# One priority per operation in place of two numbers per kind, and 20 warm-up matmuls in place of 38, in a list-scheduled kernel

## The chip, the cores and the metric

The kernel runs on one core of one Trainium2 chip. The metric is the device time of one execution in microseconds (us), and I quote medians. Most executions of one kernel agree within a per cent or so. An execution more than 1.5% above the fastest of its kernel is called slow and is left out of every ratio, though not out of the medians.

## The reference

The kernel computes a gated block on x of 2048 rows by 640 columns (S by D). One branch is a feed-forward network, 640 to 1728 to 640. The other is a convolution over all 2048 rows, done as a Fourier transform in two steps.

```python
def A_ref(q, k, v, shift_k, ssm_k, ssm_D):
    kv = shift_conv(k, shift_k) * v          # 4 taps along S
    y = irfft(rfft(pad(kv)) * rfft(pad(ssm_k)))[:S]
    return q * (y + kv * ssm_D)
def B_ref(x, w1, b1, w2, b2):
    return gelu(x @ w1 + b1) @ w2 + b2
xn = layernorm(x)
out = x + A_ref(xn, k, v, shift_k, ssm_k, ssm_D) * silu(B_ref(xn, w1, b1, w2, b2))
```

The output is x plus a small product.

## The kernel before

Nothing in the kernel is in a fixed order. While the program is built, each piece of work is handed to `plan.op` with its engine, an estimated cost, and the buffers it reads and writes. A list scheduler then plays the program on a model of the chip, and each engine's instructions are emitted in the order of the planned starts.

```python
LAT = {"PE": 0.2, "ACT": 0.15, "DVE": 0.13, "POOL": 0.15, "SP": 0.0}
MODE_SWITCH = 0.095
# ... cut
    def schedule(self):
        # ... cut: dependences and buffer slots
        for k, os in kinds.items():
            a, b = self.due[k]
            for i, o in enumerate(os):
                o.prio = -(a + (b - a) * i / max(1, len(os) - 1))
        # ... cut: for every ready operation o and every engine e it may use
                    t = max(est, free[e])
                    c = o.cost[e]
                    p = o.prio
                    # ... cut: penalties for a table load or a change of array shape
                    key = (t, -p, c)
                    if best is None or key < best[0]:
                        best = (key, o, e, t, c, slots)
        # ... cut: the winner o starts at t and ends at end
            if o.dma:
                dma_free = max(dma_free, end + 0.65) + o.dma / o.rate
                o.done = dma_free + 1.4
            else:
                o.done = end + LAT[e]
        # ... cut
        order.sort(key=lambda o: (o.start, o.i))
        return order
    def emit(self):
        for o in self.schedule():
            o.fn(o.eng)
DUE = {
    "b1": (-2658.69, -12.83), "cab0": (8557.17, 6667.77), # ... cut, a pair of numbers for each kind
}
```

The key is first the start time `t` and only then the priority, so a priority decides only between operations that could start at the same moment. All transfers share one line, first in, first out: a transfer begins when every earlier one has ended, at 330 KB per us.

The parts that the argument touches:

```python
    op("DVE", 0.14, lambda e: nc.vector.memset(b1_r[:], 0.0), writes=[b1r_b], kind="first")
    for i in range(38):   # warm-up
        op("PE", 0.22, ...matmul of 128x128 by 128x512..., kind="warm")
    def load(fn, nbytes, ...):      # at most four loads in flight: a pool of 4 tokens
    def load_rows(e):               # small loads issued by ScalarE, b1_r in two pieces
    # second half (h = 1) of k and v: lies where kT lay, so it waits for all users of kT
    def load_k(h, i): ... eng="POOL", extra=list(kT_b.users) if h else []
    def load_v(h, i): ... eng="POOL", extra=list(kT_b.users) if h else []
    # first transform step: two matmul pairs, evicted to an io tile, stored to DRAM scratch
    def f1_pair(i, h, src, src_b, scr, scr_b, kind):
        o = Buf(pool=io_pool, parts=2)               # one of four io tiles
        # ... cut: matmuls to psa buffers, evictions by ACT|DVE
        op("SP", 0.46, lambda e: nc.sync.dma_start(out=by_n2(scr[h], i), in_=o.v...), dma=P * 4 * D)
    # per group: read scratch K and U, second step (F2), product, inverse (I1)
    def middle(h, g):
        pr = [Buf(pool=io_pool) for _ in range(2)]   # the same four io tiles
        op("DVE", 0.735, prod, reads=[uin, kk[a]], writes=[pr[a]], ...)
```

The products and the stores of the first step share the four io tiles. The matmuls of the transform share three psa buffers in PSUM.

Of the kernel before, what the change touches and what calls it, by code (L numbers as in the profile page):

```python
# [64 lines left out]

LAT = {"PE": 0.2, "ACT": 0.15, "DVE": 0.13, "POOL": 0.15, "SP": 0.0}
TABLE_LOAD = 1.28
MODE_SWITCH = 0.095

class Plan:  # L70
    def __init__(self, due):
# [41 lines left out]
    def schedule(self):  # L113
        ops = self.ops
        succ = {o: [] for o in ops}
        for o in ops:
            for d in o.deps:
                succ[d].append(o)
        follow = {o: [] for o in ops}
        for o in ops:  # L120
            for d in o.after:
                follow[d].append(o)
        kinds = {}
        for o in ops:
            kinds.setdefault(o.kind, []).append(o)
        for k, os in kinds.items():
            a, b = self.due[k]
            for i, o in enumerate(os):
                o.prio = -(a + (b - a) * i / max(1, len(os) - 1))
        for o in ops:  # L130
            o.left = len(o.deps) + len(o.after)
            o.est = 0.0
            o.done = None
        free = {"PE": 1.0, "ACT": 1.0, "DVE": 1.0, "POOL": 1.0, "SP": 1.0}
        dma_free, table, mode = 0.0, None, 0
        for p in {b.pool for o in ops for b in o.allocs}:
            p.reset()
        ready = [o for o in ops if o.left == 0]
        order = []
        while ready:  # L140
            best = None
            for o in ready:
                est, slots, ok = o.est, [], True
                for b in o.allocs:
                    cand = None
                    if b.pool.fifo and b.seq != b.pool.next:
                        ok = False
                        break
                    for s in b.pool.slots:
                        if any(s is c for c in slots) or any(u.done is None for h in s[1] for u in h.users):  # L150
                            continue
                        t = max([u.done for h in s[1] for u in h.users], default=0.0)
                        if cand is None or t < cand[0]:
                            cand = (t, s)
                    if cand is None:
                        ok = False
                        break
                    est = max(est, cand[0])
                    slots.append(cand[1])
                if not ok:  # L160
                    continue
                for e in o.engs:
                    t = max(est, free[e])
                    c = o.cost[e]
                    p = o.prio
                    if e == "ACT" and o.table is not None and o.table != table:
                        c += TABLE_LOAD
                        p -= self.due["switch"][0]
                    if e == "PE" and o.mode != mode:
                        c += MODE_SWITCH  # L170
                        p -= self.due["mode"][0]
                    if e != o.engs[0]:
                        wait, less = self.due["dve" if e == "DVE" else "pool"]
                        if max(est, free[o.engs[0]]) <= t + wait:
                            continue
                        p -= less
# [3 lines that stand above are left out]
            assert best is not None, [(o.kind, o.i) for o in ready]  # L180
            key, o, e, t, c, slots = best
            for b, s in zip(o.allocs, slots):
                b.v = s[0]
                b.pool.next += 1
                s[1] = [b]
            o.eng, o.start = e, t
            end = t + c
            free[e] = end
            if e == "ACT" and o.table is not None:
                table = o.table  # L190
            if e == "PE":
                mode = o.mode
# [5 lines that stand above are left out]
            ready.remove(o)  # L198
            order.append(o)
            for s, t in [(s, o.done) for s in succ[o]] + [(s, o.start) for s in follow[o]]:  # L200
                s.left -= 1
                s.est = max(s.est, t)
                if s.left == 0:
                    ready.append(s)
        assert len(order) == len(ops), "the plan cannot run"
        order.sort(key=lambda o: (o.start, o.i))
        self.span = max(o.done for o in ops)
        return order
# [2 lines left out]
        for o in self.schedule():  # L211
            o.fn(o.eng)

DUE = {
    "b1": (-2658.69, -12.83), "cab0": (8557.17, 6667.77), "cab1": (-1486.18, -152.64), "cst0": (-305.42, 2707.06),
    "cst1": (-2821.97, -4792.38), "dve": (0.47, 30.2), "f1_0": (-871.05, 1734.66), "f1_1": (1301.71, 4641.74),
    "f1_2": (1114.17, 1732.61), "f1_3": (2717.88, 2832.21), "f1k0": (-526.64, -1917.59), "f1k1": (-45.43, 1009.63),
    "f1u0": (-4387.08, -5449.77), "f1u1": (-871.6, -2537.05), "f2_0": (-101.73, 568.69), "f2_1": (55.74, -1410.81),
    "f2_2": (2347.64, 580.24), "f2_3": (1367.74, 4253.7), "f2k0": (-4800.76, 938.43), "f2k1": (1474.47, -1695.6),
    "f2u0": (1087.17, -104.99), "f2u1": (-2201.6, -388.99), "fin0": (3005.36, 3026.91), "fin1": (4769.18, 4253.19),  # L220
    "first": (-4156.08, -3068.36), "gtab": (-2228.31, -2211.96), "halo1": (3569.33, 2410.81),
    "i10": (-236.08, -1811.7), "i11": (-1708.64, -1347.6), "i20": (2541.11, 1052.7), "i21": (2701.42, 3183.93),
    "kin0": (-593.69, 758.66), "kin1": (1951.88, -1170.69), "kt": (-677.48, -1093.47), "kv0": (-3727.38, -6497.24),
    "kv1": (818.93, -2911.39), "ln0": (-2934.3, -4187.58), "ln1": (-6791.26, -5326.47), "ln2": (1941.49, 937),
    "ln3": (896.12, -1662.13), "load1": (-2919.94, -4066.71), "load10": (1978.17, 919.81),
    "load11": (-2440.26, -3260.22), "load12": (4122.04, 8470.58), "load13": (7611.05, 3845.84),
    "load14": (3186.96, 908.54), "load15": (4188.27, 3598.3), "load16": (-1111.28, -467.99),
    "load17": (3134.69, 3049.36), "load18": (376.5, 3182.36), "load19": (1982.23, 428.93),
    "load2": (-5152.92, -6327.1), "load20": (5478.92, 7432.46), "load21": (-2345.4, 472.84),
    "load22": (-3453.91, -1273.89), "load23": (3030.08, 3625.43), "load24": (-2431.86, -3878.73),  # L230
    "load3": (-4653.66, -5026.1), "load4": (-4049.51, -2679.33), "load5": (-3127.18, -2370.67),
    "load6": (-1295.43, -2222.83), "load7": (-3086.77, -1734.57), "load8": (-486.48, 2101.2),
    "load9": (1995.94, 1552.87), "mode": (197.93, 0), "ones1": (-1676.37, -2952), "pool": (7.25, -13.8),
    "prod0": (69.2, -3781.34), "prod1": (2713.4, -508.43), "small": (-2624, 2474.77), "switch": (23.42, 0),
    "uin0": (-5019.36, -4445.98), "uin1": (-4066.58, -3058.07), "warm": (-9990.03, -8766.04),
    "wexp": (462.86, 314.56), "wtab": (-4840.89, -4511.51), "xt0": (-2587.15, -3103.92), "xt1": (191.84, -3623.5),
    "xt2": (1912.14, 2825.82), "xt3": (-3593.86, -3830.63),
}

@with_exitstack  # L240
def kernel(
# [75 lines left out]
    psf_t = [psum.tile([P, 512], F32, name="psf%d" % i) for i in range(2)]  # L317
    psa_t = [psum.tile([P, 2, 512], F32, name="psa%d" % i) for i in range(3)]

    plan = Plan(DUE)  # L320
    op = plan.op

    def evict(e, out_, in_):
# [12 lines left out]
    kf_b = Buf(parts=DT)  # L336
# [5 lines left out]
    row_b, dD_b, b1r_b, b1_b, id_b, bias_b = Buf(), Buf(), Buf(), Buf(), Buf(), Buf()  # L342
# [17 lines left out]

    warm_b = Buf()
    op("DVE", 0.2, lambda e: nc.vector.memset(hT_t[0][:, FT - 2, :], 0.0), writes=[warm_b], kind="first")
    for i in range(38):
        ps = Buf(pool=psf)
        op("PE", 0.22, lambda e, ps=ps: nc.tensor.matmul(out=ps.v[:, :], lhsT=hT_t[0][:, FT - 2, 0:P], rhs=hT_t[0][:, FT - 2, :],  # L365
                                                         start=True, stop=True),
           reads=[warm_b], writes=[ps], kind="warm")
# [16 lines left out]
    for q in range(CH):  # L384
        load(lambda e, q=q: nc.sync.dma_start(out=x_b[0].v[:, q, :], in_=x_v[:, q, :]), P * D * 2,
             writes=[x_b[0][2 * q], x_b[0][2 * q + 1]])
# [233 lines left out]
    for t in range(DT):  # L620
# [8 lines left out]
            o = ps.v[:].rearrange("p a b -> p (a b)").bitcast(BF16).rearrange("p (a b) -> p a b", b=P)  # L629
            evict(e, kT[:, h * 8:(h + 1) * 8, t * P:(t + 1) * P], o[:, h * 8:(h + 1) * 8, :])  # L630

        op("PE", 1.4, ktr, reads=[kf_b[t], id_b], writes=[ps], kind="kt")
        for h in range(2):
            op("ACT|DVE", (0.905, 0.6), lambda e, h=h, kev=kev: kev(e, h), reads=[ps],
               writes=[kT_b[2 * t + h]], kind="kt")
# [282 lines left out]
```

## Time and profile before

| | before |
|---|---|
| time, median of the first 3 runs | 211.09 us |
| profiled span | 208.5 us |
| useful TensorE work in it | 173.2 us |
| lost by 45 us (the head) | 17.7 us |
| 92 changes of array shape at 0.107 us | 9.8 us |
| other losses from 45 us to the last matmul (the body) | 3.0 us |
| tail after the last matmul | 4.8 us |

Useful work is counted as the prediction below explains it.

### The profile page before, as it was taken

What the parts mean: (1) busy time and instruction counts of PE and PEld (TensorE: products, weight loads), DVE (VectorE), ACT (ScalarE), POOL (GpSimd) and SP (SyncE); (2) the same over time, 40 slices, a digit from 0 to 9 for tenths busy, and PEclk for the clock granted to TensorE, in tenths of its full rate; (3) what the DMA queues carried; (4) which work ended last, traced back from release to release, by engine and by line L of the source; (5) the groups of instructions that cost most, each with busy time, mean ns of one, the idle gap of its engine ahead of it and who ended that gap; (6) DMA issues with size and microseconds to landing.
All of it is one profiled execution on the core that took longest, in us unless ns stands there. A gap on an engine that the chain in (4) does not pass through costs nothing.

```text
span 208.5 us, 5242 instructions
## 1 busy us (share of the span) xinstructions
PE 197.8 (95%) x2091; PEld 109.5 (53%) x2091; DVE 162.2 (78%) x301; ACT 148.2 (71%) x232; POOL 44.5 (21%) x67
## 2 busy tenths in 40 slices
PE   7997999989999999989999999999999899999990
PEld 2483446557676444334335666666643343667670
DVE  8879699999995543749899999562496676869993
ACT  2859879987787998769999776564579899830100
POOL 8992357400000001901201111001002021120000
PEclk9998899999999999999999999999999999999998
DMA  5999998993469899999964734896799963127994
GB/s 167 354 402 375 337 392 271 385 241 120 189 157 293 311 266 396 328 327 246 336 171 130 230 136 156 241 252 166 234 336 371 290 199 128 66 92 241 331 338 139
DMA packets 46137, 52.85 MB, mean 253 GB/s; under 512 B 14352, under 2 KB 35503, under 8 KB 46112
## 3 DMA queue, kind: packets, MB, share of 16 engines
q1 hardware_dynamic: 41920, 37.10, 58.0%
q0 software_dynamic: 4160, 15.40, 21.0%
q8 instruction: 16, 0.26, 0.5%
q14 instruction: 9, 0.07, 0.1%
q10 hardware_dynamic: 32, 0.01, 0.0%
HBM read 31.14 MB, written 18.35 MB: 237 GB/s over the span
## 4 chain that ended last, share of the span: by engine, by line
PE 66%; DVE 23%; DMA 6%; ACT 2%; issue 1%; SPq 0%; DVEq 0%
PE psf_105 L603 12%; PE psf_106 L603 11%; PE psf_106 L568 11%; PE psf_105 L568 9%; DVE GAB L689 5%; DVE stats L500 4%; DMA kv_90<-scrU_66 4%; DVE GAB L696 3%; DMA kv_90<-scrU_65 3%; PE psf_105 L365 3%; PE psf_106 L365 2%; PE psa_109 L851 2%; PE psa_108 L851 2%; PE psa_107 L816 2%; DVE xreg L520 2%; DVE xreg L878 2%
## 5 line engine op out<-in xcount | busy, mean ns | idle before, releaser
L568 PEld LDWEIGHTS <-w_sb 128*128 128x128 bf16 x280 | 25.1, 98 | 33.2 <-issue 9.0
L568 PE MATMUL psf_106<-hx_93,w_sb 128*128 128x512 bf16 x105 | 27.2, 391 | 0.8 <-ACT hx_93 L324 0.8
L568 PE MATMUL psf_105<-hx_93,w_sb 128*128 128x512 bf16 x105 | 26.2, 380 | 1.1 <-ACT hx_93 L573 1.1
L603 PEld LDWEIGHTS <-hx_93 128*128 128x128 bf16 x224 | 21.5, 98 | 9.4 <-issue 1.1
L603 PEld LDWEIGHTS <-hx_94 128*128 128x128 bf16 x224 | 21.7, 98 | 8.9 <-issue 0.5
L696 DVE TENSOR_TENSOR GAB<-GAB 128x1280 bf16<-128x1280 bf16 x24 | 19.6, 817 | 0.0
L603 PE MATMUL psf_105<-w_sb,hx_93 128*128 128x320 bf16 x112 | 16.6, 299 | 0.0
L603 PE MATMUL psf_106<-w_sb,hx_93 128*128 128x320 bf16 x112 | 16.6, 299 | 0.0
L603 PE MATMUL psf_105<-w_sb,hx_94 128*128 128x320 bf16 x112 | 16.6, 299 | 0.0
L603 PE MATMUL psf_106<-w_sb,hx_94 128*128 128x320 bf16 x112 | 16.5, 299 | 0.0
L858 POOL DMA_DIRECT2D scrC_67<-kv_90 x8 | 6.0, 754 | 49.0 <-ACT kv_90 L324 29.5
L500 DVE BATCH_NORM_STATS2 stats<-xreg 128x6 f32<-128x320 bf16 x32 | 13.7, 471 | 0.3 <-DMA xreg<-in_A_q_dram 0.2
L858 POOL DMA_DIRECT2D scrC_68<-kv_90 x8 | 6.0, 752 | 37.4 <-DVE kv_90 L324 15.2
L689 DVE TENSOR_TENSOR GAB<-kv_91,w_exp 128x1280 bf16<-128x1280 bf16 x16 | 13.0, 821 | 0.1
L689 DVE TENSOR_TENSOR GAB<-kv_90,w_exp 128x1280 bf16<-128x1280 bf16 x16 | 12.9, 818 | 0.0
L324 ACT CAST kv_90<-psa_108 128x640 bf16<-128x640 f32 x18 | 12.6, 701 | 0.4 <-PE psa_108 L851 0.3
L573 ACT ACTIVATE hx_93<-psf_105,b_f 128x512 bf16<-128x512 f32 (+1 forms) x14 | 9.9, 706 | 3.1 <-PE psf_105 L568 3.1
L816 PEld LDWEIGHTS <-F2m 64*32 64x32 bf16 x512 | 5.2, 89 | 12.9 <-issue 11.7
L573 ACT ACTIVATE hx_93<-psf_106,b_f 128x512 bf16<-128x512 f32 x14 | 9.8, 704 | 2.4 <-PE psf_106 L568 2.3
L324 ACT CAST kv_90<-psa_109 128x640 bf16<-128x640 f32 x15 | 10.4, 695 | 1.0 <-PE psa_108 L816 0.4
L418 POOL DMA_DIRECT2D kv_91<-in_A_v_dram x2 | 1.8, 915 | 43.2 <-ACT kk_96 L324 38.8
L573 ACT ACTIVATE hx_94<-psf_106,b_f 128x512 bf16<-128x512 f32 x14 | 9.7, 696 | 1.6 <-PE psf_106 L568 1.0
(191 smaller groups left out, 451.4 us busy)
## 6 DMA issues: line engine op xcount, KB each, us to landing
hx_94<-in_A_ssm_k_dram SPq DMA_DIRECT2D x5, 512.0 KB, 6.7
kv_90<-scrU_65 SPq DMA_DIRECT2D x8, 320.0 KB, 5.1
scrC_67<-kv_90 POOLq DMA_DIRECT2D x8, 320.0 KB, 5.5
kv_90<-scrU_66 SPq DMA_DIRECT2D x8, 320.0 KB, 4.5
kv_91<-scrC_67 SPq DMA_DIRECT2D x8, 320.0 KB, 5.0
scrC_68<-kv_90 POOLq DMA_DIRECT2D x8, 320.0 KB, 3.7
out_dram<-xreg SPq DMA_DIRECT2D x16, 160.0 KB, 4.5
kv_91<-scrC_68 SPq DMA_DIRECT2D x8, 320.0 KB, 4.8
```

The lines of the kernel that those rows point to most:

```text
L324: (nc.scalar.copy if e == "ACT" else nc.vector.tensor_copy)(out=out_, in_=in_)
L365: op("PE", 0.22, lambda e, ps=ps: nc.tensor.matmul(out=ps.v[:, :], lhsT=hT_t[0][:, FT - 2, 0:P], rhs=hT_t[0][:, FT - 2, :], start=True, st ...
L500: nc.vector.bn_stats(out=stats[:, c, j, h, :], in_=x_b[c].v[:, j, h * H:(h + 1) * H])
L520: nc.vector.tensor_scalar(out=o, in0=i, scalar1=rstd[:, c, j:j + 1], scalar2=nmr[:, c, j:j + 1], op0=ALU.mult, op1=ALU.add)
L568: nc.tensor.matmul(out=o, lhsT=w1_sb[:, t, ft * P:(ft + 1) * P], rhs=xnT_b[c].v[:, :, t, :], start=(t == 0), stop=(t == DT - 1))
L573: op("ACT", 0.575, lambda e: nc.scalar.activation(out=hT_b[c].v[0:M, ft, :], in_=ps.v[0:M, :], func=ACT.Gelu_apprx_tanh, bias=b1_f[0:M, ft ...
L603: nc.tensor.matmul(out=ps.v[:, 0:H], lhsT=hT_b[c].v[0:M, ft, q * P:(q + 1) * P], rhs=w2_sb[0:M, ft, hs], start=(ft == 0), stop=(ft == FT - 1))
L689: nc.vector.tensor_tensor(out=out_, in0=k_all[h][:, r + 3 - j:r + 3 - j + KR, :], in1=w_exp[:, j, None, hs].to_broadcast([P, KR, H]), op=A ...
L696: op("DVE", 0.735, lambda e, t=t: nc.vector.tensor_tensor(out=a.v, in0=a.v, in1=t.v, op=ALU.add), reads=[t], writes=[a], kind="kv%d" % h)
L816: nc.tensor.matmul(out=ps.v[t * 32:t * 32 + 32, r, 0:H], lhsT=F2m[r * Q:r * Q + Q, z * 32:z * 32 + 32], rhs=src[r * Q:r * Q + Q, t, :], st ...
L851: nc.tensor.matmul(out=pc[t // 2].v[r * Q:r * Q + Q, t % 2, 0:H], lhsT=I1m[t * 32:t * 32 + 32, w, :], rhs=pr[a].v[t * 32:t * 32 + 32, 2 * ...
L858: op("POOL", 0.85, lambda e: nc.gpsimd.dma_start(out=by_group(scrC[h], g), in_=cs.v), reads=[cs], writes=[scrC_b[h][g]], kind="cst%d" % h, ...
```

## The change

The intent is to give the schedule search more freedom: each operation gets its own priority, the engine of an eviction can be fixed, the cost of a change of array shape depends on the shape that is left, and the warm-up is shorter. The work itself is not touched.

```diff
-MODE_SWITCH = 0.095
+MODE_SWITCH = (0.093, 0.115, 0.137)
@@
-        kinds = {}
         for o in ops:
-            kinds.setdefault(o.kind, []).append(o)
-        for k, os in kinds.items():
-            a, b = self.due[k]
-            for i, o in enumerate(os):
-                o.prio = -(a + (b - a) * i / max(1, len(os) - 1))
+            o.prio, o.force = self.due["ops"][o.i]
@@
                 for e in o.engs:
+                    if o.force >= 0 and len(o.engs) > 1 and e != o.engs[o.force]:
+                        continue
@@
-                        c += MODE_SWITCH
+                        c += MODE_SWITCH[mode]
@@
-                    if e != o.engs[0]:
+                    if e != o.engs[0] and o.force < 0:
@@
-DUE = {
-    "b1": (-2658.69, -12.83), "cab0": (8557.17, 6667.77), ... cut
+ORDER = {
+    "dve": (1.0, 6.24), "switch": (1.83, 0.0), "pool": (9.83, -4.05), "mode": (0.98, 0.0),
+    "ops": (
+        (-29.7, -1), (-51.76, -1), (-35.76, -1), (-11.15, -1), ... cut, one pair for each operation
@@
-    for i in range(38):
+    for i in range(20):
@@
-        op("PE", 1.4, ktr, reads=[kf_b[t], id_b], writes=[ps], kind="kt")
+        op("PE", 1.0, ktr, reads=[kf_b[t], id_b], writes=[ps], kind="kt")
```

## The prediction

> **What bounds the kernel now.** I read the page's busy table and slices first, then the per-window sums, then the start times in the timeline, and last the waits. The page:
>
> ```profile
> PE 197.8 (95%) x2091; PEld 109.5 (53%) x2091; DVE 162.2 (78%) x301; ACT 148.2 (71%) x232; POOL 44.5 (21%) x67
> ...
> PE   7997999989999999989999999999999899999990
> ...
> PEclk9998899999999999999999999999999999999998
> ```
>
> TensorE (PE) is busy in every slice but the first and last, so the kernel is a TensorE queue with a head and a tail, and a new order can only save what that queue loses. Busy time hides the losses, since it counts warm-ups, cold-clock matmuls and pipelined ends. So I counted useful time from distances between starts in the timeline: FFN1 280 matmuls at 0.2157 us (60.4 us); FFN2 448 at 0.136 (60.9); the 128 WA/WB matmuls at 0.136 (17.4); the 64 GA/GB ones at 0.136 (8.7); 64 batches of eight F2 matmuls at 0.147 (9.4); 16 inverse batches at 0.55 (8.8); 80 ssm_k transposes at 0.064 (5.1); input transposes and w_exp 2.4. Together **173.1 us** of the 208.5 us span. The other 35.4 us, place by place:
>
> Head: the first useful matmul starts at 11.67 us. By 45 us only 27.2 us of useful work has been issued, so 17.8 us are lost there.
>
> ```profile
> 11.36 0.38 PE L365 MATMUL psf_106<-hx_93 128*128 128x512 bf16 x1
> ...
> 11.67 0.18 PE L490 MATMUL psf_105<-ident,b_r 14*128 14x14 bf16 x1
> ...
> 11.78 0.72 PE L626 MATMUL psa_107<-ident,hx_94 128*128 128x128 bf16 x8
> 11.88 0.17 DVE L492 CAST b_f<-psf_105 128x14 f32<-128x14 bf16 x1 [1.79 <-PE psf_105 L490]
> ```
>
> L365 is a warm-up; the tiny bias transpose L490 and the ssm_k transposes L626 stand behind all 38 of them, and even VectorE (DVE) waits 1.79 us for that transpose. The window sums show the second half of the head:
>
> ```profile
> 11.00:12.00 1.00, 1.00 (x8) 0.44 (x7) 0.12 (x2) 0.69 (x1) 1.00 (x3) 1.00 0.98 410
> 17.00:18.00 1.00, 0.57 (x8) 0.33 (x6) 1.00 (x2) 0.74 (x2) 0.20 (x1) 1.00 1.05 373
> 18.00:19.00 1.00, 0.74 (x4) 0.38 (x4) 0.97 (x4) 1.00 (x3) 0.00 (x0) 0.97 1.06 380
> 19.00:20.00 1.00, 0.34 (x1) 0.10 (x1) 1.00 (x3) 1.00 (x3) 0.00 (x0) 0.50 0.99 367
> 20.00:21.00 1.00, 1.00 (x4) 0.41 (x3) 0.97 (x4) 1.00 (x3) 0.00 (x0) 0.50 1.04 387
> ```
>
> The columns are PE, PEld, DVE, ACT, POOL, granted clock, DMA share, GB/s. TensorE starves at 17 to 20 us while the DMA engines are full; then its clock is halved from 18.9 to 22.4 us, just as FFN1 begins.
>
> Body: from 45 us to the last matmul at 203.4 us, 158.4 us pass for 145.8 us of useful work, a loss of 12.6 us. Most of it are changes of array shape:
>
> ```profile
> 69.21 0.30 PE L669 MATMUL psa_107<-kv_91,WA 128*128 128x320 bf16 x1
> ...
> 70.03 1.24 PE L568 MATMUL psf_105<-hx_93,w_sb 128*128 128x512 bf16 x5
> 71.20 0.33 PE L816 MATMUL psa_107<-kin_97,F2m 64*32 64x320 bf16 x8
> 71.35 0.32 PE L816 MATMUL psa_109<-kin_97,F2m 64*32 64x320 bf16 x8
> 71.60 0.31 PE L669 MATMUL psa_108<-kv_91,WA 128*128 128x320 bf16 x1
> ```
>
> Five FFN1 matmuls occupy 1.08 us before another full-array matmul, but 1.17 us (70.03 to 71.20) before a 64*32 one; the second F2 batch takes 0.25 us to the next full one where the first took 0.15. So about 0.10 us each way. The trace has 92 such changes; without waits I take 0.107 us each: 9.8 us. That leaves 2.8 us of true gaps in the body, waits for scrU reads among them.
>
> Tail: from 203.4 to 208.5 us, 5.1 us: SiLU, multiply, add and the last store.
>
> Check: 17.8 + 9.8 + 2.8 + 5.1 = 35.5. The measured median, 211.09 us, is 2.6 us above the span, and I keep that offset.
>
> **What the Trainium skill says.** "TensorE: Matmul & The Clock Gate", Part 1, describes a gate that grants half clock until a window of about 3.4 us has been busy, and takes it back after an idle one. The trace agrees: warm-ups start 0.43 us apart until 5.3 us and 0.216 us apart after, and the half-clock stretch lasts 3.4 us. So 20 warm-ups are enough to open the gate; what is risked is an idle window after them. The same page's Part 4 says that transposes do not count as busy for this gate; here the clock stayed at 1.00 through 48 transposes from 11.8 to 14.8 us, so this trace doesn't show it. Part 3 says that matmuls keep strict program order, which is why L490 cannot pass the warm-ups; the 1.79 us wait agrees. The skill's root page, "Trainium Kernel Development and Optimization", Key Constraints, says that DMAs issued by different engines share the same 16 DMA engines: the DMA share near 1.0 agrees, so in the head only the order of loads can help. I found no page that prices a change of array shape.
>
> **The change part by part.**
>
> 1. 18 warm-ups go. Each is 0.216 us, 3.9 us in all, so they end at about 7.7 us and not 11.6. The first ssm_k tile landed at 7.69 us (the next two at 9.40 and 10.67), and x was normalised from 12.2 us, behind VectorE's wait for L490. So some useful work can start 2 to 4 us earlier, but thinly. Estimate: 2 us.
>
> 2. The load order. In the table the three w1 loads have priorities of about 49 to 55, all loads of k and v on POOL but one about -30, the ssm_k loads -5. In the old kernel the first w1 load issued at 7.86 us and landed at 16.62, so FFN1 could not begin before then. FFN1 of chunk 0 now has priorities 3 to -41, ahead of most of the early convolution. This should fill the 17 to 20 us hole (2.6 us idle or at half clock). Against it I set a probable half-clock window after the shorter warm-up (3.4 us, costing 1.7). Estimate: net 2 us.
>
> 3. Shape changes. Corrected switch costs let the search group better. But the three psa buffers allow at most three F2 batches in a row, and the runs of F2 already average 64/33 = 1.9 batches. I take 92 down to 84: 0.8 us.
>
> 4. The rest of the order: one number per operation instead of a line per kind. Of the 2.8 us gaps and 5.1 us tail I give it 1 us. FFN2 of the last chunk and the GA/GB products carry the lowest priorities together (to -223), so the tail looks the same: one SiLU chain after TensorE's last.
>
> 5. The work itself is unchanged: 173.1 us. The forced choice of ACT or DVE for evictions moves work between engines with 71% and 78% and should cost nothing. Scheduling runs while the program is built; the ktr cost of 1.0 is only a number for it.
>
> Sum: 2 + 2 + 0.8 + 1 = 5.8 us, which I round to **6 us**: a span near 202.5 and a time of 205.0 us.
>
> **The rivals.**
>
> A. The warm-ups were hidden anyway: data, not warm-ups, set the head. For it: DMA is full from 7 to 20 us and ssm_k lands from 7.7 on. Against it: VectorE's 1.79 us wait and FFN1's late weights are matters of order. Time: about 209.5.
>
> B. The clock gate takes it back. With nothing useful from 7.7 to 11 us a window could pass idle, and two windows at half clock (3.4 us lost) cancel the gain. For it: the gate closed at 18.9 us after only one thin stretch. Time: 208 to 210.
>
> C. The plan fits its model, not the chip: the penalty for changing shape falls from 198 in a range of 18500 (1.1%) to 0.98 in a range of 278 (0.35%), so the changes could grow; 20 more would cost 2.1 us, and only 7 of the 32 F2 pairs have priorities within 1 of each other. Together with VectorE, which was busy for nearly all of 32 to 57 us, as a new bound for the convolution input, the time would be 208 to 212.
>
> D. All goes well: head lag down to 12.5 us, 76 changes, gaps 1.5, tail 4.5: span 199.7, time 202.
>
> **Range and chances.** The floor of D and rivals A to C give 201.3 to 209.2 as the range. Faster by over 2% means under 206.9 us: the 6 us must come to at least 4.2. I give that 0.63, within 2% 0.33, slower by over 2% (above 215.3) 0.04, as the body is almost gapless and little else can get worse.
>
> **What would show it.** Step 1: the first useful matmul before 9 us and no VectorE wait for L490 above 0.5 us. Step 2: the first w1 load lands before 12 us, FFN1 starts before 16 us, and useful work issued by 45 us is above 30 us (27.2 now); the clock row shows at most one half-clock window after the first. Step 3: 78 to 90 shape changes. Step 4: the last matmul within 4 to 5.5 us of the end. I am wrong if the useful work by 45 us stays near 27 us, if changes exceed 100, or if long TensorE waits appear between 45 and 200 us.

## More of the kernel before

The window sums of the kernel before, for the stretch that turns out to matter. The columns are the window, its length, busy time and instructions of TensorE (PE), its weight loads, VectorE (DVE), ScalarE (ACT) and GpSimd (POOL), then the granted clock, the share of the DMA engines, and GB/s.

```profile
85.00:90.00 5.00, 5.00 (x31) 2.18 (x30) 3.57 (x5) 3.73 (x6) 3.29 (x5) 1.00 1.02 330
90.00:95.00 5.00, 4.37 (x77) 1.61 (x75) 2.89 (x4) 3.33 (x7) 0.00 (x0) 1.00 1.16 305
95.00:100.00 5.00, 5.00 (x102) 2.16 (x87) 4.83 (x7) 4.68 (x9) 1.51 (x2) 1.00 1.09 245
```

TensorE is busy although the DMA engines are full, and the clock stays at 1.00. These are the microseconds in which the second half of k and v is loaded.

The timeline of ScalarE in the head of the kernel before (start, duration, engine, line, what, then the idle time before it and what ended it):

```profile
1.54 0.32 ACTq L379 DMA_DIRECT2D b_r<-in_B_b_dram  x1
...
5.76 2.00 ACT L467 ACTIVATE WB<-w_sb,sin_bias 128x2048 bf16<-128x2048 int32 x1 [2.27 <-DVE w_sb L465]
```

ScalarE has issued its small loads before 2.2 us, and its first table function, a table of sines, starts at 5.76.

## The result

| | before | after |
|---|---|---|
| time, median (range), 4 runs each | 210.67 us (209.30 to 211.23) | 219.55 us (217.97 to 220.67) |
| profiled span | 208.5 us | 216.2 us |
| head loss | 17.7 | 16.7 |
| shape changes | 92, 9.8 us | 82, 8.8 us |
| other body losses | 3.0 | 11.9 |
| of these, from 80 to 110 us | 1.0 | 9.3 |
| tail | 4.8 | 5.6 |

The changed kernel is **slower**: the ratio is 1.043, with a 95% interval of 1.033 to 1.052. Every ratio here is the mean time of one kernel's fast runs over that of the other's in the same rounds, so it is not quite the ratio of the quoted medians. The prediction, 205.0 us in 201.3 to 209.2, was wrong.

The loss table says where to look. The head gained 1.0 us and the shape changes 1.0, while 8.9 us were lost in the body and 0.8 in the tail. The sum, +7.7 us, is the difference of the spans. The page of the changed kernel shows the place at a glance:

```profile
PE 195.9 (91%) x2073; PEld 109.6 (51%) x2073; DVE 163.4 (76%) x301; ACT 149.7 (69%) x233; POOL 47.3 (22%) x67
...
PE   7829999999999999728999999999999999999980
...
PEclk9988999999999999995999999999999999999996
DMA  5998999669948699994469952495979995216994
```

Each digit is 5.4 us. TensorE has a hole at digits 17 and 18, counted from 0 (from 91.9 to 102.7 us), and its clock drops in the second of them. The DMA row has 9s in digits 14 to 17 and falls to 4 in digit 18, so the hole **begins while the DMA engines are full**. The windows (the columns as before):

```profile
85.00:90.00 5.00, 3.66 (x53) 1.50 (x53) 1.66 (x3) 2.92 (x6) 1.79 (x3) 1.00 1.01 351
90.00:95.00 5.00, 3.27 (x50) 1.14 (x49) 1.46 (x2) 2.65 (x4) 0.00 (x0) 1.00 1.03 395
95.00:100.00 5.00, 1.81 (x12) 0.70 (x12) 3.32 (x5) 1.27 (x2) 0.78 (x1) 0.68 0.41 143
100.00:105.00 5.00, 5.00 (x45) 1.49 (x50) 3.89 (x6) 2.05 (x5) 0.00 (x0) 0.63 0.82 212
```

TensorE, VectorE and ScalarE are all less busy than before in the first three windows. In the first two the DMA share is 1.0, so a wait for data is the first thing to look for. In the last window TensorE looks fully busy, but its clock is halved for most of it, from 96.8 to 103.7 us. The waits of TensorE, longest first (instruction, what it waited for, total us, times, longest):

```profile
PE psa_107 L918 <- DVE kv_90 L426: 4.8, 1, 4.8
PE psa_109 L728 <- ACT w_exp L426: 3.1, 1, 3.1
...
PE psa_109 L918 <- DMA kv_90<-scrU_65: 1.3, 1, 1.3
```

The second is in the head, at 15.6 us. The first is in the hole: a batch of F2 matmuls (L918) waits for VectorE's eviction (L426), which frees its psa buffer. Why was VectorE late? Its timeline, and the chain of waits around it:

```profile
96.58 0.83 DVE L942 TENSOR_TENSOR io_101<-kk_95,kv_90 128x1280 bf16<-128x1280 bf16 x1 [5.12 <-DMA scrK_64<-io_101]
97.32 0.82 DVE L426 CAST kv_90<-psa_107 128x640 bf16<-128x640 f32 x1
```

```profile
84.59 11.87 DMA scrK_64<-io_101
...
98.19 0.47 PE psa_107 L918 x8
```

This is read backwards. The F2 batch starts at 98.19, after the eviction of 97.32. The inverse matmuls (L953) had filled that psa buffer by about 92.0 us, so the eviction could have run then. But in VectorE's queue a product (L942) stands ahead of it. The product writes tile io_101, and that tile is still being stored to scratch: the store was issued at 84.59 and ran **11.87 us**. VectorE idled 5.12 us, and TensorE 4.76 us.

ScalarE can evict too, and it was idle at that time:

```profile
98.73 0.69 ACT L426 CAST kv_90<-psa_107 128x640 bf16<-128x640 f32 x1 [4.83 <-PE psa_107 L918]
```

But the eviction of 97.32 is operation 601 of the plan, and the new table fixes its engine to VectorE (its pair ends in 1). So the forced choice of the engine may be a link of this chain as well. No run moved this eviction to ScalarE, so what the choice cost is not shown.

The sum fits: 4.76 us of this wait, 1.34 us of the wait for a read of scratch U at 88.2, and the half clock from 98.2 (when TensorE has work again) to 103.7, which costs half of 5.5 us, come to 8.9 us of the 9.3 lost from 80 to 110. What a quiet store of the same size takes is told by the view of DMA issues (last number: median us to landing):

```profile
scrK_63<-io_101 SPq DMA_DIRECT2D x2, 320.0 KB, 2.2
```

What filled the DMA engines is in GpSimd's timeline:

```profile
79.33 0.88 POOL L520 DMA_DIRECT2D kv_91<-in_A_v_dram  x1
80.21 0.72 POOL L511 DMA_DIRECT2D kv_91<-in_A_k_dram  x1
...
84.10 1.81 POOL L513 DMA_DIRECT2D kv_91<-in_A_k_dram  x2 [2.58 <-PE psa_107 L771]
85.89 0.90 POOL L520 DMA_DIRECT2D kv_91<-in_A_v_dram  x1
```

All four loads of the second half of k and v (640 KB each, and 0.24 MB of halo rows) are issued within 7 us, next to the stores. The first instruction that uses them starts at 103.1 us. The DMA packets in the trace file, counted by queue from 89 to 95 us, show how the two streams shared the engines: GpSimd's queue got 460 packets and the queue of the stores and reads 489, about as many. But most of the first were of 4480 bytes, and nearly all of the second of 640 or 2560, so the loads moved 1.75 MB and everything else 0.63 MB. So far this is a theory read from one trace.

The kernel's own plan reckoned otherwise. I printed the scheduler's planned starts (no measurement, only what the kernel believes): it ends the old order at 203.2 us and the new one at 199.0, and it has this store (operation 153, for which the product waits) landing 4.6 us after issue, not 11.87. The trace of the old order runs 5.1 us behind its plan at the end, and that of the new one 17.4 us: 6.0 us behind at 82 us already, and 15.2 at 103.6.

The head has its own trouble. ScalarE in the changed kernel:

```profile
5.85 0.32 ACTq L481 DMA_DIRECT2D b_r<-in_B_b_dram  x1
8.10 0.23 ACTq L482 DMA_DIRECT2D b_r<-in_B_b_dram  x1
8.36 1.28 ACT L571 ACT_TABLE_LOAD   x1 [8.36 <-DMA hx_94<-in_A_ssm_k_dram]
9.65 2.01 ACT L571 ACTIVATE w_sb<-w_sb,turn 128x2048 f32<-128x2048 int32 x1
```

The loads that issued at 1.54 and 1.89 us now issue at 5.85 and 8.10, and the first table starts at 9.65 in place of 5.76. The listing of the compiled program shows what they wait for:

```
after:        L481 DMACopy b1_r<-in_B_b1 13x128   [waits DMAHW3_49, DVE_49]
              L482 DMACopy                        [waits DMAHW4_49]
memset first: L487 DMACopy b_r<-in_B_b_dram 13x128 [waits DVE_49]
              L488 DMACopy                        [no wait]
```

The program has eight semaphores for these transfers and uses them in turn. The memset of b1_r has gone back on VectorE (it starts at 3.48 us, 1.06 before), and the first of the loads has to wait for it too. The two loads behind it therefore come later in the count, and get semaphores that x's third load and the first ssm_k tile are still using.

### The profile page after: what moved, and what is told of

It reads as the page before. It is cut to its first block, busy times and chain, and to the rows that moved or that the text cites. A ratio compares the mean times of both kernels' runs of the same rounds, so it can differ in the third digit from the quotient of the medians.

```text
span 216.2 us, 5216 instructions
## 1 busy us (share of the span) xinstructions
PE 195.9 (91%) x2073; PEld 109.6 (51%) x2073; DVE 163.4 (76%) x301; ACT 149.7 (69%) x233; POOL 47.3 (22%) x67
## 4 chain that ended last, share of the span: by engine, by line
PE 61%; DMA 15%; DVE 11%; ACT 8%; issue 1%; SPq 1%; DVEq 0%; ACTq 0%
PE psf_105 L705 14%; PE psf_106 L705 13%; PE psf_106 L670 8%; PE psf_105 L670 8%; DMA scrK_64<-io_101 5%; DVE stats L602 4%; DMA kv_90<-scrU_66 4%; DMA kv_91<-scrC_68 3%; DMA hx_94<-in_A_ssm_k_dram 3%; PE psa_108 L771 3%; PE psa_109 L771 2%; PE psa_107 L771 2%; PE psa_107 L953 2%; DVE xreg L980 2%; PE psa_107 L918 2%; PE psa_109 L918 2%
## 5 line engine op out<-in xcount | busy, mean ns | idle before, releaser
L670 PEld LDWEIGHTS <-w_sb 128*128 128x128 bf16 x280 | 25.6, 99 | 33.0 <-issue 9.6
L670 PE MATMUL psf_106<-hx_93,w_sb 128*128 128x512 bf16 x110 | 28.5, 391 | 0.1
L670 PE MATMUL psf_105<-hx_93,w_sb 128*128 128x512 bf16 x100 | 26.0, 393 | 0.1
L426 ACT CAST kv_90<-psa_107 128x640 bf16<-128x640 f32 x17 | 11.9, 698 | 5.5 <-PE psa_107 L918 4.8
L918 PEld LDWEIGHTS <-F2m 64*32 64x32 bf16 x512 | 5.6, 90 | 17.7 <-issue 13.4
L675 ACT ACTIVATE hx_94<-psf_106,b_f 128x512 bf16<-128x512 f32 x15 | 10.4, 694 | 4.2 <-PE psf_106 L670 4.1
L426 ACT CAST kv_90<-psa_109 128x640 bf16<-128x640 f32 x17 | 11.8, 694 | 2.1 <-PE psa_108 L953 0.9
L791 DVE TENSOR_TENSOR GAB<-kv_90,w_exp 128x1280 bf16<-128x1280 bf16 x16 | 12.6, 816 | 0.0
L791 DVE TENSOR_TENSOR GAB<-kv_91,w_exp 128x1280 bf16<-128x1280 bf16 x16 | 12.6, 818 | 0.0
L675 ACT ACTIVATE hx_93<-psf_105,b_f 128x512 bf16<-128x512 f32 x15 | 10.5, 703 | 2.0 <-PE psf_105 L670 1.9
L426 ACT CAST kv_90<-psa_108 128x640 bf16<-128x640 f32 x13 | 9.1, 700 | 2.0 <-PE psa_107 L918 1.2
L675 ACT ACTIVATE hx_94<-psf_105,b_f 128x512 bf16<-128x512 f32 (+1 forms) x13 | 9.1, 697 | 1.8 <-PE psf_105 L670 1.6
```

What stands on the lines that cost most here:

```text
L426: (nc.scalar.copy if e == "ACT" else nc.vector.tensor_copy)(out=out_, in_=in_)
L670: nc.tensor.matmul(out=o, lhsT=w1_sb[:, t, ft * P:(ft + 1) * P], rhs=xnT_b[c].v[:, :, t, :], start=(t == 0), stop=(t == DT - 1))
L675: op("ACT", 0.575, lambda e: nc.scalar.activation(out=hT_b[c].v[0:M, ft, :], in_=ps.v[0:M, :], func=ACT.Gelu_apprx_tanh, bias=b1_f[0:M, ft ...
L791: nc.vector.tensor_tensor(out=out_, in0=k_all[h][:, r + 3 - j:r + 3 - j + KR, :], in1=w_exp[:, j, None, hs].to_broadcast([P, KR, H]), op=A ...
L918: nc.tensor.matmul(out=ps.v[t * 32:t * 32 + 32, r, 0:H], lhsT=F2m[r * Q:r * Q + Q, z * 32:z * 32 + 32], rhs=src[r * Q:r * Q + Q, t, :], st ...
```

## The experiments

There were two questions. **Where do the 9 us in the body come from?** Theory L says that the late loads of k and v stretch the stores, and the stall follows. Rival S is my own rival C of the prediction: the new order is bad for TensorE and VectorE whatever the transfers do. Rival W puts the blame on the shorter warm-up and the clock. **Why did the head gain 1 us and not 4?** Theory B is the memset of b1_r and its semaphores, and the rival is again W. (Whether 1 us is a gain at all is taken up under the table.)

In the edits, operations go by the numbers that the scheduler gives them: 185 to 188 are the loads of the second half (k's first rows with the halo, v's first rows, k's last rows, v's last rows); 603, 635, 619 and 651 are the first four stores of the scratch C, in time order; 1 is the memset of b1_r and 23 the small loads of ScalarE. An edit `(i, j)` takes operation i out of the planned order and puts it right behind j. Nothing else moves.

| kernel | median us | ratio to before (95%) | span | head loss | body rest | of it 80 to 110 |
|---|---|---|---|---|---|---|
| before | 210.67 | 1 | 208.5 | 17.7 | 3.0 | 1.0 |
| after | 219.55 | 1.043 (1.033 to 1.052) | 216.2 | 16.7 | 11.9 | 9.3 |
| e1_small_kv1 | 210.65 | 1.000 (0.987 to 1.014) | 211.3 | 18.4 | 5.3 | 2.1 |
| e2_kv1_late | 214.69 | 1.021 (1.011 to 1.032) | 213.3 | 18.0 | 7.8 | 4.0 |
| e3_b1_first | 216.14 | 1.028 (1.015 to 1.040) | 216.4 | 15.6 | 13.3 | 10.1 |
| e4_before_20w | 209.85 | 0.998 (0.986 to 1.010) | 207.9 | 17.1 | 2.8 | 1.3 |
| e5_both_mended | 209.70 | 0.986 (0.974 to 0.998) | 208.4 | 15.6 | 5.3 | 3.3 |
| e6_and_w1_early | 209.96 | 0.993 (0.984 to 1.002) | 207.5 | 13.1 | 6.9 | 4.0 |
| e7_dve_swap | 215.61 | 1.011 (0.996 to 1.026) | 213.6 | 17.7 | 8.4 | 5.1 |
| e8_after_38w | 218.92 | 1.032 (1.022 to 1.042) | 215.8 | 16.5 | 11.8 | 8.9 |
| e9_swap_too | 209.47 | 0.995 (0.990 to 0.999) | 207.7 | 13.2 | 6.9 | 4.5 |
| e10_all_late | 211.19 | 1.005 (0.999 to 1.010) | 209.1 | 13.2 | 8.4 | 3.8 |
| e11_old_order_mended | 215.52 | 1.020 (1.013 to 1.027) | 213.9 | 15.4 | 10.4 | 4.3 |

The median of the kernel before was 211.65 us in the rounds of e1 to e4, 211.43 in those of e5 to e8, and 210.60 in those of e9 to e11, so ratios of different rounds compare only to about a per cent. In the rounds of e1 to e4 four of its seven runs were slow, so those ratios rest on the other three. The losses are each read from one profiled run. How far they scatter can be seen in the head: the changed kernel, e1, e2 and e7 have the same order there and lose 16.7, 18.4, 18.0 and 17.7 us, with one, three, three and three windows at half clock. So the head's gain of 1.0 us over the kernel before is not resolved, nor is any other difference in the head under some 2 us. The expectations speak of losses from 80 to 105 us; I count to 110 in all kernels, so that late stalls are inside. The outputs of all kernels were accepted, also that of e1, which is wrong by construction.

### e1: the same order with fewer bytes

The changed kernel's order is kept, but the four loads fetch about 0.74 MB in place of some 2.9, so that most rows keep old data. The convolution is then wrong.

```diff
+            n = 1 if h else 8
-            nc.gpsimd.dma_start(out=k_all[h][:, 3 + 8 * i:11 + 8 * i, :], in_=k_v[:, 8 * i:8 * i + 8, hs])
+            nc.gpsimd.dma_start(out=k_all[h][:, 3 + 8 * i:3 + 8 * i + n, :], in_=k_v[:, 8 * i:8 * i + n, hs])
# v in the same way: 1 and 3 rows of the 8
```

> The changed kernel with the same order, but the four loads of the second half of k and v cut from 8 rows to 1 to 3 rows per partition (about 0.6 MB in place of 2.8 MB; the result is wrong on purpose). Theory (the burst of these loads at 79 to 86 us holds up a 320 KB store, the store holds VectorE, VectorE holds TensorE): the losses between 80 and 105 us fall from about 9 us to about 2, no half-clock stretch at 97 to 104 us, time 211 to 213 against 219.5. Rival (the stall comes from the order of VectorE and TensorE work itself, or from fewer warm-ups): within 2 us of 219.5.

The time fell to 210.65 us, a ratio of 1.000 where the changed kernel has 1.043. The loss from 80 to 110 us fell from 9.3 to 2.1. The windows (of a profiled run, 213.06 us, with its half clock at 14.1 to 24.4 us, in the head):

```profile
85.00:90.00 5.00, 3.32 (x40) 1.63 (x39) 1.39 (x2) 3.23 (x5) 1.07 (x2) 1.00 0.96 282
90.00:95.00 5.00, 5.00 (x74) 1.93 (x72) 3.80 (x6) 3.35 (x6) 0.00 (x0) 1.00 0.87 301
95.00:100.00 5.00, 4.89 (x79) 2.03 (x79) 4.90 (x8) 4.23 (x7) 0.77 (x1) 1.00 0.58 170
```

TensorE is busy again from 90 us on, with the same instructions in the same order. The chain of waits has the same store as before:

```profile
86.43 7.21 DMA scrK<-io
```

It took 7.21 us in place of 11.87. Theory L holds: the bytes make most of the stall. Rival S falls as the whole cause, since order, shapes and work of the engines are those of the changed kernel. But 7.21 us is still far from the 2.2 of a quiet store, and the window from 85 to 90 us is still thin, so some of the stall comes from the order's own stores and reads.

### e2: two of the four loads later

```diff
+        for i, after in [(186, 185), (187, 603), (188, 635)]:
+            order.remove(by[i]); order.insert(order.index(by[after]) + 1, by[i])
```

> The changed kernel, with only GpSimd's queue reordered: the first rows of k and v of the second half load first, and the two loads of the later rows (640 KB each) go out behind the first and second store of scrC. The result stays right. Theory: half the burst is gone, the stall of 4.8 us on TensorE at 93 to 98 us shrinks to under 2 us and the half-clock stretch after it vanishes; time 212 to 215. Rival (order of VectorE and TensorE): within 2 us of 219.5.

The loss from 80 to 110 us fell from 9.3 to 4.0 and the ratio to 1.021. This kernel computes the right result, so it is not only the byte count of e1 that matters but when the bytes move. The first two loads still meet the stores: TensorE waits 2.5 us for an eviction by VectorE, where I had expected less than 2. No half-clock stretch is left in the middle.

### e7: only VectorE's queue changed

The loads stay where they are. The two products that wait for io tiles go behind the two evictions (601 and 629) that stood after them.

```diff
+        for i, after in [(614, 629), (615, 614)]:
+            order.remove(by[i]); order.insert(order.index(by[after]) + 1, by[i])
```

> The changed kernel with the loads left in their burst, and only VectorE's order changed at the stall: two products that wait for the late stores go behind two PSUM evictions that were ready. If the stall is mainly that these evictions stand behind the products in an in-order queue: TensorE's wait of 4.8 us at 93 us falls below 2.5 us, time 215 to 217.5. If the transfers as such set it: the wait only moves to a later place, time within 1.5 us of 219.5.

The ratio fell to 1.011, and the loss from 80 to 110 us to 5.1. That ratio rests on two fast runs alone, 215.39 and 212.48 us, as the other two count as slow; the median of all four, 215.61 us, is 2% above the kernel before. TensorE's longest waits:

```profile
PE psa L924 <- DMA kv<-scrU: 3.3, 2, 2.8
PE psa L734 <- ACT w_exp L432: 3.1, 1, 3.1
```

The wait for VectorE's eviction is gone from the list, so the blocked queue was the link between the slow store and TensorE. But 3.3 us of waiting for reads of scratch U, through the same full DMA engines, are there in its stead, and the clock is still halved once, from 88.7 to 92.1 us. Against the 1.0 us of the kernel before, the stall was 8.3 us too large; the swap takes away 4.2 of it, and the bytes (e1) 7.2. So in these traces the transfers are the cause, and the queue order about doubled what they cost.

### e3: the memset of b1_r first

```diff
+        for i, after in [(1, 41), (23, 2)]:
+            order.remove(by[i]); order.insert(order.index(by[after]) + 1, by[i])
```

> The changed kernel with one memset (of the bias row) moved to the front of VectorE's queue, as in the old kernel, so that the four small loads on ScalarE are issued in the first microseconds and need no semaphore whose last transfer is still under way. Theory for the head (ScalarE sits behind two loads until 8.1 us, and its tables are 3 to 5 us late): the first table function starts before 7 us in place of 9.65, useful TensorE work issued by 45 us rises from 28.3 to at least 31 us; the later stall may stay; time 215 to 217.5. Rival (the head is set by the data, not by ScalarE): useful work by 45 us stays within 0.7 us of 28.3 and time within 1.5 us of 219.5.

```profile
1.54 0.32 ACTq L487 DMA_DIRECT2D b_r<-in_B_b_dram  x1
...
4.89 2.00 ACT L577 ACTIVATE w_sb<-w_sb,turn 128x2048 f32<-128x2048 int32 x1 [1.41 <-DVE w_sb L573]
```

ScalarE's loads are back at 1.54 us, the first table starts at 4.89 in place of 9.65, and TensorE's wait for w_exp falls from 3.1 to 0.8 us. Theory B holds for the late ScalarE (the edit moves the loads as well as the memset, so the two parts of the theory are not separated). The head loss falls to 15.6 us, from the 16.7 to 18.4 of the four traces with the changed kernel's head; useful work by 45 us is then 29.4 us, short of the 31 that I had expected. The ratio falls from 1.043 to 1.028, but the intervals overlap. The loss from 80 to 110 us is 10.1, so the stall in the middle is still there; this was read from the slowest of the four runs (218.19 us, the median is 216.14), so that it grew is not shown.

### e4 and e8: the warm-up alone

e4 is the kernel before with 18 of its warm-up matmuls left out, and e8 the changed kernel with 18 added behind its last one.

```diff
# e4
+            if o.i not in range(23, 41):
                 o.fn(o.eng)
# e8
+            if o.i == 14:          # the last planned warm-up matmul
+                self.more()        # 18 more
```

> The old kernel with its old order, and only 18 of the 38 warm-up matmuls left out. My prediction's step 1: 1 to 2 us faster than before, the first useful matmul near 7.8 us. Rival A (data sets the head): within 0.7 us of before. Rival B (the clock gate closes after the shorter warm-up): 1.5 to 4 us slower, with a half-clock stretch between 8 and 20 us.

> The changed kernel with 38 warm-up matmuls again (the other part of the change undone). If the shorter warm-up is what made it slower: back to 210 to 213, with no half-clock stretch before 25 us. Theory (the order is the cause; the first ssm_k transposes now wait until 11.6 us, but the chain behind ScalarE is later still): within 1.5 us of 219.5, the losses between 80 and 105 us still 7 us or more.

e4 has a ratio of 0.998: its first useful matmul starts at 7.84 us in place of 11.67, but the head loss falls only from 17.7 to 17.1. e8 has 1.032 against 1.043 of the changed kernel; the intervals overlap, and the head losses are 16.5 and 16.7. Rival W falls both ways: 18 warm-ups more or less move nothing that these runs resolve, and e8 still loses 8.9 us from 80 to 110 us. Part of what the shorter warm-up saves is paid back at half clock: e8 has no half-clock stretch before 25 us, whereas most kernels with 20 have one to three windows of 3.4 us there (from 14.9 to 18.3 us in the changed kernel, from 13.7 to 24.0 in e2, although both have the same order in the head). e4 has two such windows (15.7 to 22.5 us) and the kernel before has one.

### e5, e6 and e9: the repairs together

```diff
# e5: e3, and three loads behind stores of scratch C
+ [(1, 41), (23, 2), (186, 603), (187, 635), (188, 619)]
# e6: e5, and the first load of w1 right behind GpSimd's last start-up memset
+ [(30, 43)]
# e9: e6, and the swap of e7
+ [(614, 629), (615, 614)]
```

> The changed kernel with two moves and nothing else: the bias memset at the front of VectorE's queue, and in the second half's loads only k's first rows left in the burst, the other three loads (640 KB each) behind the first, second and third store of scrC. Theory (two causes, the blocked ScalarE in the head and the burst at 79 us): the losses between 80 and 105 us, 9.3 us in the changed kernel, fall to 2 to 4; useful work by 45 us is 29 us or more; time 208.5 to 212, so level with the old kernel. Rival (something else in the new order costs the time): over 214.

> As the run with both moves, and the first w1 load moved ahead of the index tables on GpSimd (it issued at 8.1 us and landed at 17.2 us in the changed kernel). If FFN1's start waits for those weights: first FFN1 matmul 1 to 3 us earlier and time 1 to 2 us below the run with both moves. If the transposed x is what FFN1 waits for, or the earlier load delays x: within 1 us of it, or slower.

> The changed kernel with the bias memset first, the first w1 load early, three of the four late loads behind scrC stores, and VectorE's two products behind the two ready evictions: all mends so far together. If the losses of the two causes add up: TensorE's 1.6 us wait for VectorE at 90 us goes, useful work by 45 us about 32 us, time 207 to 209, 1 to 2 % below the old kernel. If the gains of the head are taken back in the middle, as in the run with early w1: 209.5 to 210.5.

With both repairs the ratio is 0.986 (0.974 to 0.998), where the changed kernel has 1.043. So these two repairs recover the whole loss in time, although the body is still 2.3 us worse than before; a shorter head and fewer shape changes pay for that. e6 cuts the head loss by another 2.5 us, to 13.1, and has no half-clock stretch from the end of its warm-up to its last matmul. But the body gives back 1.6 us, and the ratio, 0.993, is no better within the intervals. e9, timed in five rounds, has 0.995 (0.990 to 0.999): it is faster than the kernel before by half a per cent, which the interval only just tells from nothing and which is far inside the 2% within which two kernels count as the same. Its 209.47 us lies between the two branches of its expectation, at the edge of the one in which the middle takes back what the head gains. It is the best supported of the versions that beat both kernels; e5's lower ratio comes from three noisier rounds.

### e10 and e11: is "later" a rule?

e10 is e9 with all four loads behind stores of scratch C, k's first rows too. e11 puts the lessons on the **old** order: 20 warm-ups, the first load of w1 early, and the loads of k and v spread out.

```diff
# e10
+ [(185, 603), (186, 635), (187, 619), (188, 651)]   # in place of e9's three
# e11, on the kernel before (its numbers are 18 higher)
+ [(203, 202), (204, 653), (205, 637), (206, 621), (48, 67)]   # and 18 warm-ups dropped
```

> As the run with all mends, and the load of k's first rows (900 KB with the halo) also behind the first scrC store. If that load is what still holds up the stores at 78 to 90 us: losses between 75 and 105 us fall by another 1 to 2 us, time 206 to 208. If VectorE's work on the second half, which waits for these rows, becomes late: no gain, or 1 to 2 us slower.

> The old kernel's order with 20 warm-ups, the first w1 load early and three of the four late loads behind scrC stores. Theory: the old order lost only 1.4 us between 80 and 105 us, so the late loads give at most 1 us; the head gains 1 to 3 us; time 206.5 to 209.5. If the head's gain is taken back later, 210 to 211.

Both were no gain. e10 is at 1.005; its head is as good as e9's, but the body loses 8.4 us. e11 is slower than the kernel before, 1.020 (1.013 to 1.027; whether by over 2% is open), outside both branches of what I had expected. Its longest wait:

```profile
PE psa L822 <- DMA kin<-scrK: 4.9, 2, 3.3
```

The longer of the two, 3.3 us, ends at 107.9 us: the loads, moved off the stores (three are issued from 94.6 to 100.9 us), now meet a read of scratch K, and the clock is halved from 106.7 to 113.5 us. Part of this lies beyond the stretch that I count, so the column of 80 to 110 us shows less. e11 made three changes at once, so this reading is from its trace, not isolated. Still, the rule is not "spread the loads". A load placed where the plan sees room can meet a read that TensorE needs at once. The old order had the same loads at 78.2 to 87.4 us and lost 1.0 us. Why exactly it bears them so well I did not isolate: the trace shows its store of scrK_64 from io_100 taking 7.0 us (84.15 to 91.13), with TensorE fully fed meanwhile. SyncE issued no other transfer between that store and 92.01 us, whereas the changed kernel had issued a read at 82.35 us and another store at 85.19, around the one that stretched. That this is the reason, or that the products there happened not to stand ahead of an eviction, is argued, not shown.

## Why the prediction was wrong

**Part 4 failed, "the rest of the order".** I gave it a gain of 1 us, since the body was almost gapless. It cost 8.9 us in the body, nearly all of it from 80 to 110 us. The reasoning "little else can get worse" read a gapless body as a property of the work. It was a property of the old order. The sum of my four parts, 5.8 us, needed a body that stays gapless under a new order, and that was the claim with nothing behind it.

**Rival C named the danger but not the mechanism.** "The plan fits its model, not the chip" is what happened: the plan promised 4.2 us (203.2 to 199.0). But I looked for the misfit in the shape changes and in VectorE as a bound, and gave it little weight: 0.04 for slower. The shape changes behaved, and VectorE was idle when it hurt. The misfit is in the transfers. The model serves one transfer after another; the chip mixes them. The Trainium skill, "DMA: Bandwidth & Descriptors", section "Queues, rings and completion order", says that each DMA engine goes round the queues that have work, packet by packet. The trace agrees: equal counts of packets for the two queues from 89 to 95 us (460 and 489), and 11.87 us for a store against 2.2 for quiet ones; in e1, with fewer bytes in the other queue, it took 7.21. I had read of the sharing, and drew only a conclusion about the head from it. I had also misread the table: I gave all loads of k and v but one priorities of about -30, but the four of the second half, which made the burst, stand at -103.

**Part 1, warm-ups, 2 us:** the first useful matmul came at 8.12 us, before 9 as foretold. But e4 isolates this part, and its head loss falls by 0.6 us, within the scatter. Rival A (the warm-ups were hidden anyway) and B (the clock takes it back) are both in that number. At the bias transpose, L490 before and L592 after, there is still a wait: VectorE waits 1.37 us for it, where I had said at most 0.5, because TensorE itself now waits 1.1 us there for the b1 load.

**Part 2, load order, 2 us:** it failed. The first w1 load issued at 8.10 us and landed at 17.20; I had said before 12, and before the change it was 16.62. FFN1 began at 21.1 us and not before 16. I read high priorities as early issue. But a priority only breaks ties between equal start times, GpSimd is busy with its start-up work until 8.1 us, and at most four loads are in flight. Useful work by 45 us was 28.3 us, not above 30. The semaphore wait of ScalarE, which no view of the kernel before could show, took some 1 to 3 us more (e3, against the four traces with the same head). e6 shows that the early load was worth 2.5 us in the head, had the order contained it.

**Part 3, shape changes:** right. I said 84 and 0.8 us; the trace has 82, so 10 fewer, which is 1.1 us.

**Part 5** said that the forced choice of the engine for evictions should cost nothing. The eviction in front of the hole was forced to VectorE while ScalarE idled 4.83 us; what that cost was not measured.

**The tail** lost 5.6 us, just outside my 4 to 5.5. The sign that I had set for being wrong, "long TensorE waits between 45 and 200 us", is what appeared: 4.76 us at 98.

## What to carry to other kernels

A schedule searched on a model should be checked first where the model is crudest, and in this kernel that was concurrent transfers: compare planned and measured times of landing under load, not the engines' durations. An instruction that may wait for a transfer should not stand in an in-order queue ahead of one that frees a buffer for the bound engine. And a gain in the head of a kernel counts only if a later stall does not absorb it: e6's head was 2.5 us shorter than e5's, its body gave back 1.6 us, and the ratio was no better.

## What the Trainium skill lacked or had wrong

- "DMA: Bandwidth & Descriptors" describes how queues share the engines, but gives no figure for how far an ordinary transfer is stretched by others of the same core. Here a 320 KB store took 11.87 us under a DMA share of 1.0, 7.21 with most of the other queue's bytes taken away, and 2.2 when quiet.
- The same page, in "Why a DMA increments its semaphore by 16 and not by 1", warns of two transfers in flight that share one semaphore. It does not say what the cure costs: a program that uses eight in turn and waits for each to come free issued two small loads at 5.85 and 8.10 us in place of 1.54 and 1.89 (up to 3.6 us the first waited for a memset), and held ScalarE's first table until 9.65 us.
- No page prices a change of array shape between matmuls. Here 92 or 82 changes of about 0.107 us each fit the spans.
- "TensorE: Matmul & The Clock Gate", Part 1, says that the window of the gate is free-running and lasts about 3.4 us. The runs agree in the length. It gives the change from run to run for the first matmuls of a kernel; a thing to add is that later windows differ too. With one and the same order in the head, one profiled run spent a single window at half clock (14.9 to 18.3 us, the changed kernel) and another three (13.7 to 24.0, e2); the head losses were 16.7 and 18.0 us.
